# Attention: where the guard's checks of a blocked inverse stand, which engine copies a first column, and who writes two diagonal blocks

## The chip, the core and the metric

The program runs on one core of a Trainium2 chip. The metric is the device time of one execution in microseconds (us). The engines named below are TensorE (PE, with its weight loads PEld), VectorE (DVE), ScalarE (ACT), GpSimd (POOL) and SyncE (SP, which issues most of the DMAs). Each engine works through its own instructions in the order in which they stand.

## The reference

Three layers follow each other. The change lies in the first, a recurrence over 768 steps for 4 x 8 heads with a 40x40 state each; its outputs are routed, token by token, to one of 8 experts, and a dense layer with a leaky activation ends it.

```python
# _attn_ref: r, k, v, w, a, b are [4, 8, 768, 40]
for t in range(S):
    y[:, :, t] = np.einsum('bhd,bhde->bhe', rt, state)
    Sa = np.einsum('bhde,bhe->bhd', state, at)
    state_decay = state * wt[:, :, None, :] - np.einsum('bhd,bhe->bhde', Sa, bt)
    state = state_decay + np.einsum('bhd,bhe->bhde', vt, kt)
# _moe_ref: x is y as [3072, 320]
logits = x @ w_gate; expert_idx = np.argmax(logits, axis=1)   # gate = softmax at the argmax
out[mask] = gate_w[mask, None] * (np.maximum(x[mask] @ w1[e], 0.0) @ w2[e])   # for each expert e
# _moe2_ref
h = x @ w_in
return (np.maximum(h, 0.0) + alpha * np.minimum(h, 0.0)) @ w_out
```

## The kernel before

The recurrence is computed in chunks of 64 steps. Four chunks (256 steps) of two batches form a *group*; there are six groups, `os[0]` to `os[5]`. For a group, `prepare` loads w, k, b and a for a quarter of it at a time (four calls a group, 24 in all), takes products of the decays by two scans on DVE (lines 465 and 467, with a reciprocal at 466 between them), and scales k, b and a. The first column of the first scan's result, 104x8 numbers, is kept in `s0` for the step from one chunk to the next; a copy on ACT (line 471) does that. `products` multiplies the scaled tiles on PE (`lp`, line 494), and ACT copies the result into `l1` and `l2`. `inverse` then inverts the 64x64 triangular matrices of the group: their 32x32 diagonal blocks by 31 steps on DVE in the tile `ut` (lines 551 and 553), two transposes on DVE into `ttc` and `t11` (lines 573 and 576), and the blocks off the diagonal by two rounds of matmuls, `zp` (line 597) and `yp` (line 607). The result T is put together in the tile `tt`, a half of the group at a time. `diagonal` copies the diagonal blocks from `ttc` into `tt` (line 569, four instructions a half), on POOL, but on DVE for the first half of the first group. ACT copies `zp` into `z` (line 601) and `yp` into `tt` (line 610, "the copies of T"). The first group has eight small matmuls on a tile of ones ahead of each `zp` and each `yp` (`fill`).

A guard watches whether the numbers stay in a safe range. `check` squares a tile on ACT with an accumulator: one instruction and a short one that reads the accumulator. For each group `inverse` checks `ut` and then `l1`, ahead of the second half (lines 587 and 588); the first writes its squares over `ut`, the second into `ttc`. `ut` is also read by the transpose into `t11`, so its check waits for that.

The chunks themselves run in 48 *slots*, eight a group. In a slot, PE multiplies T into the sides (`pp`, line 649), ACT copies that (`pw`, line 651), PE makes `sa` (line 689), ACT and DVE copy it to `va` (lines 691 and 694), PE makes `yc` (line 705), DVE takes the next state `sm` from it (lines 709 and 710), PE transposes that (`tp`, line 716), and ACT copies it to `bds` (line 717). The next group's `prepare`, `products` and `inverse` are laid among the slots of the group before, by a table in `run`: a group's first half of T is needed in its first slot, its second half four slots on.

What stands where on each engine is decided by a scheduler that places instructions by modelled times, except in the first stretch, where DVE, POOL and ACT keep the order of the code (`manual_schedule`, closed by `self.region.close()`). `issue_after` tells the scheduler to place an instruction behind another.

Of the kernel before, what the change touches and what calls it, by code (L numbers as in the profile page):

```python
# [13 lines left out]
AF = mybir.ActivationFunctionType  # L14
ALU = mybir.AluOpType
# [273 lines left out]
class Attention:  # L289
# [148 lines left out]
    def prepare(self, o, pg):  # L438

        nc = self.nc  # L440
        nw = 2 * NCS * CW
        half, bb = divmod(pg, 2)
        p4 = slice(4 * bb, 4 * bb + 4)
        if pg == 0:
            o.s0 = self.p.tile([PP, 8, NCS], F32, name="s0", bufs=4)
            o.group, o.q, o.la, o.kbr = {}, {}, {}, {}
        if bb == 0:
            o.q[half] = self.p.tile([PP, 8, 2, CW], F32, name="q", bufs=5)
        kbs, abds = (self.kb_start, self.abd_start) if o.start else (self.kb, self.abd)
        wz, ra, kb, abd = (self.ringed(*n) for n in (("wz", self.wz), ("ra", self.ra), ("kb", kbs), ("abd", abds)))  # L450
        for q in range(2):
            r = slice(q * HQ, q * HQ + D)
            nc.sync.dma_start(wz[r], self.wP[o.bp, o.g, pg, q])
            nc.sync.dma_start(kb[r].rearrange("p a x t -> p (a x t)"), self.kbP[o.bp, o.g, pg, q])
            nc.sync.dma_start(ra[r].rearrange("p a t -> p (a t)"), self.aP[o.bp, o.g, pg, q])
        w3 = wz[:, :nw].rearrange("p (c t) -> p c t", t=CW)[:, :, 1:]
        s = self.pa.tile([PP, nw], F32, name="s", bufs=2)
        s3 = s.rearrange("p (c t) -> p c t", t=CW)
        qt = o.q[half][:, p4]
        qc = qt.rearrange("p a c t -> p (a c) t")  # L460
        if o.start:
            self.check(w3, self.pa.tile([P, 2 * NCS, C], F32, name="junk", tag="t4", bufs=3)[:PP], 1.24, self.mid)
        else:
            self.check(w3, qc[:, :, :C], 1.24, self.mid)
        nc.vector.tensor_tensor_scan(s[:, ::-1], wz[:, 1:][:, ::-1], self.d1s[:, ::-1], 0.0, ALU.mult, ALU.max)
        nc.vector.reciprocal(self.d1q.rearrange("p (c t) -> p c t", t=CW)[:, :, 0], s3[:, :, 0])
        nc.vector.tensor_tensor_scan(qt.rearrange("p a c t -> p (a c t)"), wz[:, :nw], self.d1q, 0.0, ALU.mult, ALU.max)  # L467
        for x in range(2):
            eng = nc.vector if o.start else nc.gpsimd
            eng.tensor_tensor(kb[:PP, :, x, :], kb[:PP, :, x, :], s3[:, :, 1:], op=ALU.mult)  # L470
        nc.scalar.copy(o.s0[:, p4, 2 * half:2 * half + 2], s3[:, :, 0].rearrange("p (a c) -> p a c", c=2))
        for q in range(2):
            r = slice(q * HQ, q * HQ + D)
            nc.gpsimd.tensor_tensor(abd[r, :, q * C:(q + 1) * C], ra[r], qc[r, :, :C], op=ALU.mult)  # L474
        o.group[pg] = abd.rearrange("p (a c) t -> p a c t", c=2), kb.rearrange("p (a c) x t -> p a c (x t)", c=2)
# [50 lines left out]
    def inverse(self, o):  # L526

        nc = self.nc
        l1, l2 = o.l1, o.l2
        o.tt = [self.ringed("tt", self.tt) for _ in range(2)]  # L530
        ut = self.ut0 if o.start else self.unit()
        ul = self.pa.tile([P, 32, 32], F32, name="ul", tag="t4", bufs=3)
        nc.vector.transpose(ul, l2.rearrange("p c u j -> p j (c u)"))
        yield
        for j in range(31):
            n, m = 31 - j, j + 1
            if o.start:
                if j == 0:
                    tmp = self.pa.tile([P, 1024], F32, name="tmp", tag="t4", bufs=3)
                col = ul[:, j, j + 1:]  # L540
            else:
                if j == 0:
                    bank = self.work("tmp", [P, 512], "mg")
                    tmp = bank[:, :256]
                if j in (0, 8, 16):
                    j0, j1 = j, (8, 16, 32)[j // 8]
                    part = bank[:, 256:256 + (j1 - j0) * (32 - j0)].rearrange("p (a b) -> p a b", b=32 - j0)
                    nc.scalar.copy(part, ul[:, j0:j1, j0:])
                col = part[:, j - j0, j + 1 - j0:]
            tv = tmp[:, :n * m].rearrange("p (a b) -> p a b", b=m)  # L550
            nc.vector.tensor_tensor(tv, col.unsqueeze(2).to_broadcast([P, n, m]),
                                    ut[:, j, :m].unsqueeze(1).to_broadcast([P, n, m]), op=ALU.mult)
            nc.vector.tensor_tensor(ut[:, j + 1:, :m], ut[:, j + 1:, :m], tv, op=ALU.subtract)  # L553
            if j % 2:
                yield

        lows = [slice(q * 64, q * 64 + 32) for q in range(2)]
        highs = [slice(q * 64 + 32, q * 64 + 64) for q in range(2)]

        def vacant(half):  # L560
            if not o.start:
                for lo, hi in zip(lows, highs):
                    nc.gpsimd.memset(o.tt[half][lo, :, :, hi], 0.0)

        def diagonal(half):
            for q in (1, 3, 0, 2):
                r = slice(32 * q, 32 * q + 32)
                eng = nc.vector if o.start and half == 0 else nc.gpsimd
                eng.tensor_scalar(o.tt[half][r, :, :, 32 * q:32 * q + 32], ttc[r, 2 * half:2 * half + 2], 1.0, 0.0, op0=ALU.mult, op1=ALU.add)

        vacant(0)
        ttc = self.t4("ttc")
        nc.vector.transpose(ttc.rearrange("p c u t -> p t (c u)"), ut)
        diagonal(0)
        t11 = self.t4("t11")
        nc.vector.transpose(t11.rearrange("p c u s -> p s (c u)"), ut.rearrange("p t s -> p s t"))
        yield

        pairs = [(c2, u) for u in range(8) for c2 in range(2)]
        out = lambda t, c2, q: t[c2 * 64:c2 * 64 + 32, :, q * 32:q * 32 + 32]  # L580
        heads = lambda t: t.rearrange("p (q s) -> p q s", q=2)
        wide = lambda t, c, u: t.rearrange("p c u j -> p (c u j)")[:, 32 * (8 * c + u):min(32 * (8 * c + u) + C, 1024)]
        for half in range(2):
            if half:
                vacant(1)
                diagonal(1)
                self.check(ut, ut, 0.01)
                self.check(l1.rearrange("p c u j -> p (c u) j"), ttc.rearrange("p c u t -> p (c u) t"), 0.01)
                yield
            tt = o.tt[half]  # L590
            zp = self.work("zp", [P, 8, C], "mg" if o.start or half == 0 else "w1")
            if o.start:
                self.fill(zp, 8)
            for c2, u in pairs:
                w = wide(l1, 2 * half + c2, u)
                high = heads(tt[:, c2, u])[:, :, 32:]
                nc.tensor.matmul(heads(zp[c2 * 64:c2 * 64 + w.shape[1], u]), lhsT=w, rhs=high, start=True, stop=True)
            z = self.z
            for c2 in range(2):
                for q, lo in enumerate(lows):  # L600
                    nc.scalar.copy(z[lo, c2, :, q * 32:q * 32 + 32], out(zp, c2, q))
            yp = self.work("yp", [P, 8, C], "mg" if o.start or half == 0 else "w1")
            if o.start:
                self.fill(yp, 8)
            for c2, u in pairs:
                w = wide(t11, 2 * half + c2, u)
                nc.tensor.matmul(yp[c2 * 64:c2 * 64 + w.shape[1], u], lhsT=w, rhs=z[:, c2, u, :], start=True, stop=True)
            for c2 in range(2):
                for q, (lo, hi) in enumerate(zip(lows, highs)):
                    nc.scalar.activation(tt[lo, c2, :, hi], out(yp, c2, q), AF.Copy, scale=-1.0)  # L610
            yield


# [767 lines left out]
```

## Time and profile before

| | |
|---|---|
| Device time, median of 3 runs | 1084.41 us (1084.05 to 1087.19) |
| The profiled execution | 1090.49 us, its span 1088.8 us |
| PE busy in the span | 980.7 us (90%) |
| DVE / ACT / POOL busy | 681.9 / 536.5 / 490.9 us |

The span is from the first to the last instruction of one execution. An engine is busy while an instruction of it runs, and idle while the next one waits; each wait is put down to the instruction that ended last before it, its releaser. The attention's inverse of the first group ends near 100 us, the 48 slots run to about 480 us, and the experts and the dense layer fill the rest.

### The profile page before, as it was taken

To read this page: it belongs to the slowest core of one execution; us is meant where nothing else is said; L and a number is where in the kernel's file an instruction comes from. 1 tells how busy PE (TensorE), PEld (TensorE's weight loads), DVE (VectorE), ACT (ScalarE), POOL (GpSimd) and SP (SyncE) were. 2 spreads that over 40 slices of the span, in tenths; PEclk is the share of its full clock that TensorE was granted. 3 is DMA by queue.
4 is the path that set the end of the run, shared out by engine and by line. 5 is a ranking of instruction groups with operands and counts; after the bars stand their busy time and mean duration, and the time that the engine had idled before them with its cause. 6 is when DMAs were issued, how large, how long until landed. Compare 5 with 4: busy or idle time off the path is not lost. (4 is left out here: it accounts for less than half of the span.)

```text
span 1088.8 us, 24353 instructions
## 1 busy us (share of the span) xinstructions
PE 980.7 (90%) x9213; PEld 871.9 (80%) x9213; DVE 681.9 (63%) x1493; ACT 536.5 (49%) x1303; POOL 490.9 (45%) x571
## 2 busy tenths in 40 slices
PE   2669987888879998887999999999999999999997
PEld 2557776777668777776899999899898988988986
DVE  9795968868978695556899753243444444344533
ACT  4657766686677777645677544421212222222211
POOL 7766677785867645320000003524435343534332
PEclk8669999999999999898999999999999999999999
DMA  4462323333323234427999643410000000000000
GB/s 121 103 204 72 93 73 81 90 77 83 89 77 84 55 68 105 111 55 262 324 332 321 212 149 106 124 46 7 19 25 25 25 25 25 26 25 25 25 1 28
DMA packets 128320, 103.33 MB, mean 95 GB/s; under 512 B 90564, under 2 KB 111044, under 8 KB 128196
## 3 DMA queue, kind: packets, MB, share of 16 engines
q1 hardware_dynamic: 125892, 93.83, 30.1%
q0 software_dynamic: 2304, 7.87, 2.3%
q8 instruction: 75, 1.23, 0.5%
q14 instruction: 49, 0.40, 0.1%
HBM read 79.39 MB, written 22.28 MB: 93 GB/s over the span
## 5 line engine op out<-in xcount | busy, mean ns | idle before, releaser
L234 POOL TENSOR_TENSOR gl<-g,gh 128x512 fp32r<-128x512 f32 x96 | 123.6, 1290 | 216.4 <-ACT gh L233 124.8
L233 ACT ACTIVATE gh<-g 128x512 fp32r<-128x512 f32 x96 | 60.8, 633 | 251.9 <-DVE g L1268 178.2
L1267 DVE TENSOR_SCALAR g<-ph,al 128x512 f32<-128x512 f32 x96 | 72.1, 751 | 160.1 <-POOL gl L234 77.6
L243 PE MATMUL ph<-x2thi,win 128*128 128x512 f32 x480 | 159.5, 397 | 0.0
L243 PE MATMUL po<-wout,gh 128*128 128x320 f32 x768 | 139.0, 310 | 0.0
L243 PEld LDWEIGHTS po<-wout,gh 128*128 128x128 f32 x768 | 122.0, 188 | 5.6
L243 PE MATMUL ph<-x2tlo,win 128*128 128x512 f32 x288 | 114.3, 397 | 0.0
L243 PEld LDWEIGHTS ph<-x2thi,win 128*128 128x128 f32 x480 | 88.6, 188 | 14.9
L243 PE MATMUL po<-we,hh 128*128 128x320 f32 (+1 forms) x480 | 92.5, 322 | 6.8 <-ACT hh L1137 6.1
L243 PE MATMUL ph<-xthi,we 128*128 128x448 f32 (+2 forms) x360 | 97.5, 342 | 0.1
L1076 POOL TENSOR_TENSOR win<-raw,win 128x1024 fp32r<-128x1024 f32 x4 | 9.6, 2406 | 185.3 <-ACT win L1074 185.2
L243 PEld LDWEIGHTS po<-we,hh 128*128 128x128 f32 (+1 forms) x480 | 75.9, 187 | 10.7 <-ACT hh L1137 6.7
L243 PE MATMUL po<-wout,gl 128*128 128x320 f32 x384 | 82.9, 312 | 0.0
L243 PE MATMUL ph<-xtlo,we 128*128 128x448 f32 (+2 forms) x216 | 73.7, 342 | 0.9 <-DVE xtlo L276 0.9
L494 PE MATMUL lp<-kb,abd 128*128 128x128 f32 x352 | 58.2, 309 | 17.2 <-POOL abd L474 10.3
L474 POOL TENSOR_TENSOR abd<-ra,q 40x512 f32<-40x512 f32 x44 | 61.4, 1396 | 22.4 <-DVE q L467 12.3
L243 PEld LDWEIGHTS ph<-xthi,we 128*128 128x128 f32 x360 | 66.5, 195 | 3.3 <-ACT xthi L273 0.2
L1268 DVE SCALAR_TENSOR_TENSOR g<-ph,g 128x512 f32<-128x512 f32 x96 | 66.3, 691 | 3.1
L243 PEld LDWEIGHTS po<-wout,gl 128*128 128x128 f32 x384 | 64.0, 188 | 3.0
L494 PEld LDWEIGHTS lp<-kb,abd 128*128 128x128 f32 x352 | 49.1, 212 | 21.6 <-POOL abd L474 10.8
L553 DVE TENSOR_TENSOR ut<-ut,tmp 128x31 f32<-128x31 f32 (+15 forms) x186 | 62.5, 336 | 3.6
L689 PE MATMUL sa<-vg,pw 128*64 128x104 f32 x768 | 57.2, 262 | 6.8 <-issue 4.6
(217 smaller groups left out, 2241.5 us busy)
## 6 DMA issues: line engine op xcount, KB each, us to landing
raw<-in_moe_w_dram SPq DMA_DIRECT2D x16, 512.0 KB
raw<-in_moe_w_dram SPq DMA_DIRECT2D x16, 480.0 KB
kb<-in_kbP_dram SPq DMA_DIRECT2D x44, 160.0 KB
r<-in_moe_w_in_dram SPq DMA_DIRECT2D x10, 512.0 KB
r<-in_moe_w_out_dram SPq DMA_DIRECT2D x10, 512.0 KB
xs_d<-tt SPq DMA_DIRECT2D x8, 560.0 KB
raw<-in_moe_w_dram SPq DMA_DIRECT2D x16, 256.0 KB
wz<-in_wP_dram SPq DMA_DIRECT2D x48, 81.4 KB
```

What stands on the lines that cost most here:

```text
L233: nc.scalar.activation(hi, src, AF.Copy)
L234: return lo_eng.tensor_tensor(lo, src, f32(hi), op=ALU.subtract)
L243: return nc.tensor.matmul(out, lhsT=lhsT, rhs=rhs, start=start, stop=stop)
L474: nc.gpsimd.tensor_tensor(abd[r, :, q * C:(q + 1) * C], ra[r], qc[r, :, :C], op=ALU.mult)
L494: nc.tensor.matmul(lp[:, i], lhsT=abd[:, i, c2, :], rhs=kb[:, i, c2, :], start=True, stop=True)
L553: nc.vector.tensor_tensor(ut[:, j + 1:, :m], ut[:, j + 1:, :m], tv, op=ALU.subtract)
L689: nc.tensor.matmul(sa[q * 64:q * 64 + 64, i], lhsT=x.pw[:, i, q * C:(q + 1) * C], rhs=x.vg[:, i, q, :], start=True, stop=True)
L1076: eng.tensor_tensor(wt[:, 3 + c, cs], raw, f32(wt[:, c, cs]), op=ALU.subtract)
L1267: nc.vector.tensor_scalar(g, ph, 0.0, al[:, f:f + 1], op0=ALU.min, op1=ALU.mult)
L1268: nc.vector.scalar_tensor_tensor(g, ph, 0.0, g, op0=ALU.max, op1=ALU.add)
```

## The change

The copy of the first column goes from ACT to DVE, between the reciprocal and the second scan. Of the four diagonal blocks of the first half of the first group, ACT writes two and DVE two. The two checks leave the start of the second half: the check of `ut` is placed behind the copies of T of the first half, that of `l1` behind those of the second, which now writes its squares over `l1`. The `fill` ahead of `yp` goes.

```diff
         nc.vector.reciprocal(self.d1q.rearrange("p (c t) -> p c t", t=CW)[:, :, 0], s3[:, :, 0])
+        nc.vector.tensor_copy(o.s0[:, p4, 2 * half:2 * half + 2], s3[:, :, 0].rearrange("p (a c) -> p a c", c=2))
         nc.vector.tensor_tensor_scan(qt.rearrange("p a c t -> p (a c t)"), wz[:, :nw], self.d1q, 0.0, ALU.mult, ALU.max)
...
-        nc.scalar.copy(o.s0[:, p4, 2 * half:2 * half + 2], s3[:, :, 0].rearrange("p (a c) -> p a c", c=2))
...
                 r = slice(32 * q, 32 * q + 32)
-                eng = nc.vector if o.start and half == 0 else nc.gpsimd
-                eng.tensor_scalar(o.tt[half][r, :, :, 32 * q:32 * q + 32], ttc[r, 2 * half:2 * half + 2], 1.0, 0.0, op0=ALU.mult, op1=ALU.add)
+                to, src = o.tt[half][r, :, :, 32 * q:32 * q + 32], ttc[r, 2 * half:2 * half + 2]
+                if o.start and half == 0 and q % 2:
+                    nc.scalar.copy(to, src)
+                else:
+                    eng = nc.vector if o.start and half == 0 else nc.gpsimd
+                    eng.tensor_scalar(to, src, 1.0, 0.0, op0=ALU.mult, op1=ALU.add)
...
-                self.check(ut, ut, 0.01)
-                self.check(l1.rearrange("p c u j -> p (c u) j"), ttc.rearrange("p c u t -> p (c u) t"), 0.01)
...
-            if o.start:
-                self.fill(yp, 8)
...
-                    nc.scalar.activation(tt[lo, c2, :, hi], out(yp, c2, q), AF.Copy, scale=-1.0)
+                    done = nc.scalar.activation(tt[lo, c2, :, hi], out(yp, c2, q), AF.Copy, scale=-1.0)
+            with self.tc.issue_after(done.ins):
+                src = l1.rearrange("p c u j -> p (c u) j") if half else ut
+                self.check(src, src, 0.01)
```

The scheduler lays all instructions anew, so the order moves beyond these lines. ACT in the first group, before, from the check of `ut` on (`s` is the first column, `tt_127` the first half of T):

```order
L434 ACTIVATE ut,checks_134<-ut 128x1024
L471 COPY s_1447<-s 104x4x2
L601 COPY z_120<-zp 32x8x32 x4
L434 ACTIVATE ttc,checks_134<-l_183 128x1024
L495 COPY l_617<-lp 128x128
L496 COPY l_618<-lp 128x128
L515 COPY kbr<-bp 128x320
L679 COPY vg_410<-rp 40x4x64 x2
L681 COPY rs<-rp 104x256
L471 COPY s_1447<-s 104x4x2
L610 ACTIVATE tt_127<-yp 32x8x32 x4
```

The same place now, from the two diagonal blocks on (line 609 holds the copies of T):

```order
L570 COPY tt_127<-ttc 32x16x32 x2
L603 COPY z_120<-zp 32x8x32 x4
L495 COPY l_608<-lp 128x128
L496 COPY l_609<-lp 128x128
L515 COPY kbr<-bp 128x320
L609 ACTIVATE tt_127<-yp 32x8x32 x4
L434 ACTIVATE ut,checks_134<-ut 128x1024
L521 ACTIVATE la<-ap 64x4x40 x2
```

Ahead of the copies to `z` two blocks of T stand instead of a check and a column; ahead of the copies of T a check, a column and the copies of `rp` are gone; behind them a check has come.

ACT at the end of a later group's inverse (the third), before:

```order
L434 ACTIVATE ut,checks_134<-ut 128x1024
L691 COPY va_409<-sa 64x4x40 x2
L515 COPY kbr<-bp 128x320
L601 COPY z_120<-zp 32x8x32 x4
L521 ACTIVATE la<-ap 64x4x40 x2
L717 COPY bds_417<-tp 104x208
L662 COPY vg_412<-rvp 64x4x64 x2
L434 ACTIVATE ttc,checks_134<-l_1482 128x1024
L495 COPY l_2583<-lp 128x128
L496 COPY l_2584<-lp 128x128
L610 ACTIVATE tt_128<-yp 32x8x32 x4
```

And now:

```order
L694 COPY va_409<-sa 64x4x40 x2
L515 COPY kbr<-bp 128x320
L603 COPY z_120<-zp 32x8x32 x4
L521 ACTIVATE la<-ap 64x4x40 x2
L720 COPY bds_417<-tp 104x208
L665 COPY vg_412<-rvp 64x4x64 x2
L609 ACTIVATE tt_128<-yp 32x8x32 x4
L434 ACTIVATE ut,checks_134<-ut 128x1024
L495 COPY l_2568<-lp 128x128
L496 COPY l_2569<-lp 128x128
L515 COPY kbr<-bp 128x320
L654 COPY pw_422<-pp 104x512
```

One check has gone from ahead of `va` and `z` to between the copies of T and the slot's `pw` (line 654); the check of `l1` has left this place. DVE at the end of the first group's inverse now:

```order
L577 STREAM_TRANSPOSE ttc<-ut 128x32x32
L580 STREAM_TRANSPOSE t_513<-ut 128x32x32
L573 TENSOR_SCALAR tt_127<-ttc 32x16x32 x2
L465 SCALAR_TENSOR_TENSOR s<-wz_106,d1s_117 104x520
L466 RECIPROCAL d1q_122<-s 104x8
L467 COPY s_1432<-s 104x4x2
L468 SCALAR_TENSOR_TENSOR q<-wz_106,d1q_122 104x520
```

Two blocks of the diagonal stand here where four stood, and the copy of the column has come ahead of the second scan, here and at each of the other calls of `prepare`.

## Rows read from the trace of the kernel before

**Rows 1.** Busy time by stretch: us, busy of each engine (instructions), PE clock, DMA share, GB/s.
```profile
0.00:77.25 77.25, 38.55 (x200) 32.92 (x201) 67.16 (x120) 40.76 (x101) 53.79 (x70) 0.71 0.51 151
77.25:102.80 25.55, 24.42 (x348) 21.19 (x349) 13.83 (x18) 17.09 (x53) 17.23 (x19) 0.89 0.21 58
102.80:475.00 372.20, 323.18 (x5222) 274.77 (x5220) 287.70 (x801) 263.07 (x762) 243.82 (x350) 0.98 0.34 83
```

**Rows 2.** Waits of PE from 102 to 475 us: us in total, times, longest.
```profile
PE tp L716 <- DVE sm L710: 15.9, 18, 1.9
...
PE yp L607 <- ACT z L601: 3.3, 3, 2.6
...
PE pp L649 <- ACT bds L717: 1.4, 1, 1.4
```

**Rows 3.** Timeline, end of the first inverse: start, us, instruction [idle before <-releaser].
```profile
71.20 1.95 DVE L573 STREAM_TRANSPOSE ttc<-ut 128x1024 f32<-128x1024 f32 x1
...
74.90 4.21 DVE L569 TENSOR_SCALAR tt<-ttc 32x512 f32<-32x512 f32 x4
...
77.25 1.97 PE L597 MATMUL zp<-tt,l 128*64 128x64 f32 x32 [7.29 <-DVE tt L569]
...
80.71 0.20 ACT L471 COPY s<-s 104x8 f32<-104x8 f32 x1 [4.69 <-DVE s L465]
80.82 1.51 ACT L601 COPY z<-zp 32x256 f32<-32x256 f32 x4
...
83.04 0.62 PE L243 MATMUL yp<-ones 128*128 128x128 bf16 x8
83.59 1.15 PE L607 MATMUL yp<-z,t 128*64 128x64 f32 x32
...
86.39 0.20 ACT L471 COPY s<-s 104x8 f32<-104x8 f32 x1 [0.61 <-DVE s L465]
86.50 1.54 ACT L610 ACTIVATE tt<-yp 32x256 f32<-32x256 f32 x4
```

**Rows 4.** Waits of ACT from 102 to 475 us.
```profile
ACT s L471 <- DVE s L465: 25.1, 13, 3.2
...
ACT ut L434 <- DVE t L576: 9.3, 4, 2.7
```

**Rows 5.** Timeline, ACT and PE at the end of the third group's inverse.
```profile
221.77 1.15 PE L597 MATMUL zp<-tt,l 128*64 128x64 f32 x32 [1.03 <-POOL tt L569]
...
222.10 1.06 ACT L434 ACTIVATE ut<-ut 128x1024 f32<-128x1024 f32 x1 [2.60 <-DVE t L576]
...
224.21 1.52 ACT L601 COPY z<-zp 32x256 f32<-32x256 f32 x4
...
226.21 1.11 PE L607 MATMUL yp<-z,t 128*64 128x64 f32 x32
...
227.26 1.06 ACT L434 ACTIVATE ttc<-l 128x1024 f32<-128x1024 f32 x1
...
228.74 1.54 ACT L610 ACTIVATE tt<-yp 32x256 f32<-32x256 f32 x4
...
231.46 0.58 ACT L651 COPY pw<-pp 104x512 f32<-104x512 f32 x1 [0.23 <-PE pp L649]
```

**Rows 6.** Durations by line: ns min/median/max, first and last start, forms.
```profile
L434 ACT ACTIVATE ut<-ut x6: 1008/1058/1059, 74.9 to 415.3; 128x1024 f32<-128x1024 f32 x6
L434 ACT ACTIVATION_READ_ACCUMULATOR ut<-ut x6: 185/186/194, 75.8 to 416.3; 128x1 f32 x6
L466 DVE RECIPROCAL d1q<-s x24: 153/196/207, 5.9 to 344.5; 104x8 f32<-104x8 f32 x24
L974 DVE TENSOR_SCALAR over<-sl x12: 151/222/457, 151.4 to 481.8; 128x2 f32<-128x2 f32 x12
L569 DVE TENSOR_SCALAR tt<-ttc x4: 739/1056/1305, 74.9 to 78.4; 32x512 f32<-32x512 f32 x4
L324 ACT COPY vv<-zero x2: 626/628/630, 34.4 to 35.8; 128x512 f32<-128x512 f32 x2
```

## The prediction

> **What bounds the kernel now.** I read the busy times by stretch first. Up to 77.25 us DVE is busy for 67.16 us of 77.25 and PE for only 38.55: the scans and the 31 steps of the first inverse on DVE set the pace. From there to 102.8 us PE is busy 24.42 of 25.55 us, so PE is nearly full. From 102.8 to 475 us no engine is: PE has 323.18 of 372.2 us, DVE 287.70, ACT 263.07 [rows 1]. In this stretch, the slots, each engine waits for another in turn. The waits of PE come second: the largest is for DVE's state `sm`, 15.9 us in 18 times; for ACT there are smaller ones, the copies to `z` 3.3 us and `bds` 1.4 us [rows 2]. So a stall on ACT costs something only where ACT stands between two matmuls that wait for it. The waits of ACT come third: 25.1 us in 13 times for the first scan, ahead of the copy of the column, and 9.3 us in 4 times for the transpose into `t11`, ahead of the check of `ut` [rows 4]. Both are instructions at the head of ACT's queue whose own result nobody needs soon; what stands behind them waits with them. Behind 480 us PE's matmuls are the chain, and the change does not touch them: what the attention gains or loses is carried to the end.
>
> **First group.** The transpose into `ttc` ends at 71.20 + 1.95 = 73.15 us, and `zp` starts at 77.25, behind DVE's first two blocks, which stand behind the second transpose [rows 3]. Now ACT writes these two, and it is idle then. The nearest row for such a copy is 0.63 us (128x512, half of whose lanes it needs) [rows 6], so two take 1.26 and `zp` may start near 74.5. But eight of the new DVE copies stand ahead of `ttc` (four calls of `prepare` for the first group, four for the second). The nearest row is the reciprocal on the same 104x8 numbers, 0.196 us [rows 6]: 8 x 0.2 = 1.6 us, all on the DVE path. `zp` comes 4.1 - 1.26 - 1.6, about 1.2 us, earlier. Then the copies to `z`: `zp` ends at 79.22, they start at 80.82, because a column copy waited 4.69 us for a scan: 1.6 us that go. `yp` ends at 84.74, the copies of T start at 86.50, again behind a column copy: 1.76 us that go [rows 3]. Together 4.5 us. PE can't give so much: in the stretch to 102.8 us it idles 25.55 - 24.42 = 1.1 us, and the two fills ahead of `yp` save 2 x 0.62 [rows 1, 3]. So the bound is 1.2 + 1.1 + 1.2 = 3.5 us. The check of `ut`, 1.06 + 0.19 = 1.25 us [rows 6], stands ahead of the first slot's `pw` now, and both halves of T ahead of the first `va`. I take -2.5 us, with 0 and -4.5 as ends. The fills had covered a wait of PE; `lp` and `bp`, which stand between `zp` and `yp` in the new order, are the cover that is left.
>
> **The ends of the five other inverses.** The one at 222 us shows the pattern. `zp` ends at 222.92; the check of `ut`, which had waited 2.60 us for the transpose, ends near 223.25, and `z` starts at 224.21, 1.29 us late. `yp` ends at 227.32; the check of `l1`, from 227.26, holds the copies of T until 228.74, 1.42 us late [rows 5]. With both checks gone T comes up to 2.7 us earlier. Then the check of `ut` stands between T and `pw`, which takes 1.25 us of it back: 1.45 us earlier at `pw`, and that only if PE, which is also full at these places, follows. At the other ends the lateness is smaller or PE's order sets `yp`. I take half, 0.7 us, five times: -3.5 us. The ends: -13.5 (2.7 each) and +6 (each check adds its 1.25 ahead of `pw` and what stood before it had been hidden).
>
> **The check of l1 behind the second half of T.** It does not vanish: 1.25 us now stand ahead of `va` or `bds` of the slot in which the second half is finished, five times, 6.3 us at most. Where a column copy waited at the same place, up to 3.2 us [rows 4], the room is there already. I take +1 us, from 0 to +6.3.
>
> **The column copies in the slots.** On ACT 13 waits of 25.1 us go [rows 4]. But what stands behind them (`bds`, `vg`, `pw`) mostly meets PE or DVE waiting for that same scan. Of PE's waits for ACT the row on `bds`, 1.4 us, is one that a column copy causes; the others are a few tenths. I take -1.5 us, from 0 to -6. On DVE 16 copies come, 16 x 0.2 = 3.2 us, between the reciprocal and the scan that `abd`, and so `lp`, wait for. DVE is busy for 287.70 of 372.2 us [rows 1]; I put half of it on the path: +1.6 us.
>
> The price of that copy is not shown. It is bounded by the reciprocal (0.196) below. Above, by rows in which a DVE instruction on SBUF data is stretched: the four blocks of 32x512 took 0.739 to 1.305 us, a 128x2 tensor_scalar 0.151 to 0.457 [rows 6]. I take 0.2, the row of the same shape; at 1.3 us the 16 copies would be 21 us and the eight ahead of `ttc` 10. The Trainium skill, in "SBUF — State Buffer", section "Who interferes with whom", says that a copy whose source and target lie in SBUF can take the second pair of ports, which VectorE shares with GpSimd, and that whichever of the two starts first blocks the other for its whole instruction. The spread of the four blocks agrees with it, and no run here shows a copy of 104x8. By it the sum would go the way of the fourth case below.
>
> **The sum.** -2.5 - 3.5 + 1 - 1.5 + 1.6 = -4.9 us. The profiled execution took 1090.49 us, 1.69 more than its span; that becomes 1085.6. The median of the runs shown is 6.08 us below the profiled execution, so the forecast for the median is 1079.5 us. The case's own range, with half to one and a half of the gain, is 1077 to 1082.
>
> **The rivals.**
> Second: more comes. If the slots are bound by the exchange between ACT and DVE, in which ACT waits for a scan and DVE for ACT's copies, then the ends of the inverses give their 1.45 us each in full (7.3), the first group its bound of 3.5, and the column copies 1.5 more: -12 us, 1072. For it: both rows of [rows 4] are larger than all of PE's waits for ACT. Against: PE's largest wait is for DVE's `sm` [rows 2], and DVE gets more work.
> Third: no change. The slots' chain goes through DVE's `sm` and through PE, which is busy for 87% of the stretch; what the ends of the inverses win is waited off at the next `sm`, and the check that now stands ahead of `pw` takes the rest. The first group's 2.5 us are met by the 3.2 us of DVE copies: 1084.4. Against: the first group's stretch is PE's, and the fills are simply gone.
> Fourth, slower: the new copy on DVE is held by POOL, which is busy for 243.82 of 372.2 us with instructions that read SBUF [rows 1]. At the median of the four blocks, 1.06 us [rows 6], each copy costs 0.86 us more than counted. In the 71 us ahead of `ttc` DVE is the path, so the eight give 6.9 us there; of the 16 others, 13.8 us, I put a quarter on the path, 3.4. With the -4.9 of the sum that is +5.4 us: 1089.8. It decides from a mean copy of about 0.6 us on. Against: the reciprocal just ahead of it on the same numbers is never above 0.207 us, and the scan behind it would meet POOL anyway, so that part of such a wait is only moved.
> That the change doesn't do what it says is ruled out for the order: both checks stand behind the copies of T, and no column copy is left on ACT.
>
> **How the numbers follow.** Forecast 0.45, second 0.13, third 0.22, fourth 0.20. What can be told from no change is about 0.3%, 3.3 us. The forecast lies at -4.9, so a part of it, 0.03, falls into "same": faster 0.55; same 0.23, with a little of the third case going either way; slower 0.22. The range takes in the second case and nearly all of the fourth: 1070 to 1090.
>
> **What would show it.** In the trace after: the two blocks on ACT near 0.6 us each and `zp` of the first group near 76 us; `z` straight behind `zp` and T straight behind `yp`, in all six groups; no wait of ACT ahead of a check; DVE copies near 0.2 us; the first `sm` 2 to 3 us earlier than now and the last near 5. The forecast is wrong if the DVE copies take 0.6 us or more, if `pw` behind the check comes later against T than it did, or if the first `sm` is earlier but the last is not.

## The result and the profile after

The changed kernel is slower. Six runs of it have a median of 1090.35 us (1087.92 to 1093.47), six of the kernel before 1085.70 us (1082.55 to 1089.43). The ratio is 1.0051, with a 95% interval of 1.003 to 1.0072. A second measurement, below, gives 1.0044. All ratios are taken over the fast runs of the two kernels and are not quotients of the medians, from which they differ by up to 0.17%. The forecast was 1079.5 us. The fourth case, the new DVE copy held by POOL, had 1089.8.

The two traces would tell the opposite: the profiled execution of before took 1090.49 us, more than any of its six timed runs, and that of after 1087.92 us, the least of its six. So what follows takes places and durations from the traces, and the price from the medians.

The busy times by stretch, of after, answer to [rows 1]; the columns are the same.

```profile
0.00:77.25 77.25, 38.30 (x200) 32.72 (x200) 67.89 (x125) 39.03 (x92) 49.20 (x67) 0.73 0.49 145
77.25:102.80 25.55, 23.34 (x325) 20.55 (x327) 14.10 (x21) 18.51 (x53) 20.07 (x20) 0.81 0.21 60
102.80:475.00 372.20, 325.58 (x5235) 277.87 (x5231) 291.58 (x816) 263.52 (x750) 248.52 (x352) 0.97 0.35 84
```

In the second stretch PE is busy for 1.08 us less than before, but that does not tell whether its work came earlier: the two fills that are gone had 0.62 us each, and a second trace of the kernel before (e8, below) has 23.42 us there. The timeline of after at the end of the first inverse, which answers to [rows 3], tells more.

```profile
73.89 1.91 DVE L577 STREAM_TRANSPOSE ttc<-ut 128x1024 f32<-128x1024 f32 x1
...
75.25 0.72 ACT L434 ACTIVATE q<-wz,mid 104x512 f32<-104x512 f32 x1 [1.94 <-DMA wz<-in_wP_dram]
...
76.90 1.24 ACT L570 COPY tt<-ttc 32x512 f32<-32x512 f32 x2
...
78.20 1.98 PE L599 MATMUL zp<-tt,l 128*64 128x64 f32 x32 [5.54 <-ACT tt L570]
...
80.22 1.52 ACT L603 COPY z<-zp 32x256 f32<-32x256 f32 x4 [2.08 <-PE zp L599]
...
82.30 0.85 DVE L467 COPY s<-s 104x8 f32<-104x8 f32 x1
...
83.62 1.98 PE L607 MATMUL yp<-z,t 128*64 128x64 f32 x32
...
85.64 1.53 ACT L610 ACTIVATE tt<-yp 32x256 f32<-32x256 f32 x4 [1.49 <-PE yp L607]
87.20 1.01 ACT L434 ACTIVATE ut<-ut 128x1024 f32<-128x1024 f32 x1
```

The handovers are as the edit meant them: `z` starts 0.04 us after `zp` ends (78.20 + 1.98), and T as closely behind `yp`. But `ttc` starts 2.69 us later than before. ACT's two blocks, 0.62 us each, wait another 1.1 us behind two checks of `q` that a DMA had held up. So `zp` starts 0.95 us later than before instead of 1.2 us earlier. In the second trace of the changed kernel (e1) the two blocks do not wait for a check, and `zp` starts at 76.95 us; but `ttc` is late there too, at 73.63.

The waits of ACT and of PE from 102 to 475 us, of after; they answer to [rows 4] and [rows 2].

```profile
ACT va L694 <- PE sa L692: 17.8, 32, 1.1
ACT l L495 <- PE lp L494: 13.3, 13, 1.4
ACT bds L720 <- PE tp L719: 11.5, 12, 2.4
```

```profile
PE tp L719 <- DVE sm L713: 18.7, 15, 3.3
...
PE yp L607 <- ACT z L603: 2.2, 4, 1.2
```

ACT's 25.1 us ahead of the column copy and 9.3 us ahead of the checks are gone. ACT now waits for PE instead. PE waits 18.7 us for DVE's `sm`, 2.8 us more than before; in the second traces it is 16.8 (e1) against 14.7 (e8). The durations, of after, which answer to [rows 6]:

```profile
L466 DVE RECIPROCAL d1q<-s x24: 152/198/207, 5.9 to 342.7; 104x8 f32<-104x8 f32 x24
...
L467 DVE COPY s<-s x24: 120/271/2449, 6.1 to 318.7; 104x8 f32<-104x8 f32 x24
...
L570 ACT COPY tt<-ttc x2: 614/616/618, 76.9 to 77.5; 32x512 f32<-32x512 f32 x2
```

The 24 DVE copies of 104x8 numbers take from 0.12 to 2.45 us, 10.59 us in all, a mean of 0.44. Eight of them, 4.95 us, lie ahead of `ttc`.

### The profile page after: what moved, and what is told of

It reads as the page before. It is cut to its first block, busy times and chain, and to the rows that moved or that the text cites. A ratio compares the mean times of both kernels' runs of the same rounds, so it can differ in the third digit from the quotient of the medians.

```text
span 1086.2 us, 24314 instructions
## 1 busy us (share of the span) xinstructions
PE 981.8 (90%) x9197; PEld 873.7 (80%) x9197; DVE 686.1 (63%) x1515; ACT 536.8 (49%) x1281; POOL 493.8 (45%) x571
## 3 DMA queue, kind: packets, MB, share of 16 engines
q8 instruction: 75, 1.23, 0.5%
## 4 chain that ended last, share of the span: by engine, by line
PE 50%; DMA 2%; DVE 1%; ACT 1%; SPq 0%; issue 0%; POOL 0%; DVEq 0%; ACTq 0%
PE ph L243 24%; PE po L243 24%; PE tr_ps L270 2%; DMA raw<-in_moe_w_dram 2%; DMA raw<-w_out 0%; ACT wout L1093 0%; DVE we L1094 0%; DMA xs_d<-xr,sli 0%; POOL wout L1094 0%; ACT we L1077 0%; SPq L1076 0%; DVE dec L216 0%; SPq L1055 0%; ACT hh L1140 0%; DVE xtlo L274 0%
## 5 line engine op out<-in xcount | busy, mean ns | idle before, releaser
L494 PE MATMUL lp<-kb,abd 128*128 128x128 f32 x352 | 60.7, 319 | 16.0 <-DVE s L467 9.5
L494 PEld LDWEIGHTS lp<-kb,abd 128*128 128x128 f32 x352 | 51.7, 222 | 20.1 <-POOL abd L474 10.7
L243 PEld LDWEIGHTS ph<-x2tlo,win 128*128 128x128 f32 x288 | 54.2, 188 | 9.5
```

The source lines that it names most:

```text
L243: return nc.tensor.matmul(out, lhsT=lhsT, rhs=rhs, start=start, stop=stop)
L494: nc.tensor.matmul(lp[:, i], lhsT=abd[:, i, c2, :], rhs=kb[:, i, c2, :], start=True, stop=True)
```

## Experiments

The theories were these. A: the column copy on DVE is the price, since it is held while POOL works. B: the checks cost it, since they now stand between T and `pw` or `va`. C: leaving out the filling products on `yp` costs PE's clock. D: it is scatter. Others (E to H) are named where they come in. Each run was timed in five rounds beside the kernel before, except e8, which ran once.

| run | what it is | median us | ratio to before | 95% interval |
|---|---|---|---|---|
| e1 | the changed kernel again | 1092.64 | 1.0044 | 1.0020 to 1.0067 |
| e2, e12 | before + column copy on DVE | 1096.98, 1098.59 | 1.0083, 1.0081 | 1.0053 to 1.0114, 1.0048 to 1.0113 |
| e3 | before + checks behind T | 1088.05 | 0.9997 | 0.9973 to 1.0022 |
| e4 | before + two blocks on ACT, no fill | 1092.75 | 1.0018 | 0.9991 to 1.0046 |
| e5, e13 | as e2, a reduction for the copy | 1087.97, 1091.02 | 1.0023, 1.0007 | 1.0001 to 1.0045, 0.9987 to 1.0026 |
| e6 | changed, a reduction for the copy | 1087.87 | 1.0014 | 0.9995 to 1.0033 |
| e7, e16 | changed, column copy on ACT | 1082.28, 1081.77 | 0.9976, 0.9975 | 0.9954 to 0.9997, 0.9953 to 0.9997 |
| e9 | as e2, copy in the first 8 only | 1094.10 | 1.0030 | 1.0008 to 1.0052 |
| e10 | as e2, copy in the last 16 only | 1093.81 | 1.0026 | 1.0003 to 1.0049 |
| e11, e17 | as e7, with the fill on `yp` | 1085.68, 1081.24 | 0.9950, 0.9977 | 0.9926 to 0.9975, 0.9958 to 0.9996 |
| e14 | changed, with the fill on `yp` | 1091.45 | 1.0000 | 0.9978 to 1.0023 |
| e15 | before without the fill on `yp` | 1082.63 | 0.9981 | 0.9959 to 1.0003 |

The medians of before lie between 1084.87 and 1090.93 us from one set of runs to the next, so only ratios are compared across sets.

### e1 to e4: again, and one edit at a time

e1, no edit:

> The changed kernel once more, unaltered, beside the kernel before on the same chip. Theory A (the cost is real and sits in the edits): again 3 to 7 us above the kernel before. Theory D (the ratio of the first six runs, 1.003 to 1.0072, is scatter from run to run): within 0.3%, that is within 3 us. A second trace also tells which stretches repeat: under A the first tt copy again starts about 73.9 us and the column copies on DVE again take a mean of about 0.4 us with one or more above 1 us.

e2, against before:

```diff
+        nc.vector.tensor_copy(o.s0[:, p4, ...], s3[:, :, 0]...)   # behind the reciprocal
-        nc.scalar.copy(o.s0[:, p4, ...], s3[:, :, 0]...)          # behind the kb products
```

> The kernel before with one edit only: the first column of s is copied on DVE between the reciprocal and the scan, not on ACT. Theory A (a DVE copy is held while POOL works, and it stands ahead of the scan): 3 to 6 us slower than the kernel before, mean copy above 0.35 us, the first tt copy 2 to 3 us later than 71.2 us. Theory B (the place of the checks costs it): no change, within 2 us. My prediction's own step: 1.5 us faster to 1.6 us slower, with copies of 0.2 us.

e3, against before:

```diff
-                self.check(ut, ut, 0.01)          # behind diagonal(1)
-                self.check(l1..., ttc..., 0.01)
+            with self.tc.issue_after(done.ins):   # behind the copies of T
+                self.check(src, src, 0.01)
```

> The kernel before with one edit only: the two checks stand behind the copies of T. Theory B (the check now lies between the copy of T and what ACT does next, pw and va): 2 to 5 us slower than the kernel before. Theory A: 1 to 4 us faster, since only the gain of the shorter end of the inverse is left (my prediction's step: 2.5 us faster), and the waits of the check for DVE's t (9.3 us before) are gone.

e4, against before:

```diff
+                if o.start and half == 0 and q % 2:
+                    nc.scalar.copy(to, src)
-            if o.start:
-                self.fill(yp, 8)
```

> The kernel before with one edit only: in the first group ACT writes two of the four diagonal blocks, and the filling products on yp are left out. Theory C (without the filling products PE's granted clock falls in 77 to 103 us, 0.81 against 0.89): 1 to 3 us slower, first sm later than 102.8 us. My prediction's step: 1 to 3 us faster, zp near 75 us. Theory A and theory B: within 2 us of the kernel before.

The slowdown repeats, so D falls. Of the single edits only the column copy is slower than before beyond its interval, by 9 us, which is more than the whole change and more than the 3 to 6 us of A. B falls but for its lowest edge: the checks alone give 0.9997, at most 1.0022, that is 2.4 us. In e3 the gain that A and the forecast expected is not seen; the forecast's 2.5 us lie just inside the interval. e4 does not tell.

### e5, e6, e12, e13: is it the copy's form, or its place in the order?

A reduction over an axis of one element writes the same column. The order of every engine's instructions stays that of the twin with the copy, row for row; only these 24 instructions differ. e5 and e13 are e2 with it, e6 is the changed kernel with it, e12 is e2 again.

```diff
-        nc.vector.tensor_copy(o.s0[:, p4, ...], s3[:, :, 0]...)
+        nc.vector.tensor_reduce(o.s0[:, p4, ...], s3[:, :, 0:1]..., axis=AX.X, op=ALU.max)
```

> As the run with the column copy alone on DVE, whose order on all five engines it keeps row for row, but the column is written by a reduction over an axis of one element instead of a copy. Theory A (the copy's own stalls beside POOL are the cost): the 24 instructions take 0.12 to 0.2 us each, worst below 0.4 us, the first tt copy starts 1.5 to 2 us earlier than the 73.15 us of the copy, and at least half of that run's 0.83% is gone: 1.000 to 1.004 of the kernel before. Theory E (the new order alone costs it, whatever the instruction takes): 1.006 to 1.010 again. Theory F (any instruction at that place is held, by what POOL does, not by the form of the copy): the reduction too has a mean above 0.35 us and one above 2 us.

> The changed kernel with the same exchange: a reduction writes the column, the order on all five engines is that of the changed kernel row for row. Theory A: the changed kernel's 1.0044 falls to 0.997 to 1.001 of the kernel before, since only the copy's stalls were dear. Theory E: 1.003 to 1.006 again.

> The column copy alone on DVE once more, now beside its reduction twin on the same chip, since the halves (1.003 and 1.0026, against 1.0023 with no copy) do not add up to the 1.0083 first measured. Theory A (the held copies are the price, some 0.6%): 1.006 to 1.009. Theory H (the first measurement was high, the copies cost about 0.1 to 0.3% and the new order the rest): 1.003 to 1.0055.

> Its twin with the reduction, same order on all engines. Theory A and theory H both: 1.000 to 1.0045 as before; what counts is the distance to the copy's run on the same chip: 0.4 to 0.7% by A, 0.1 to 0.3% by H.

The same stretch of the twins: first DVE and POOL of e12, with the copy.

```profile
35.52 2.28 POOL L376 MEMSET vg<- 128x832 f32 x3
36.48 0.17 DVE L466 RECIPROCAL d1q<-s 104x8 f32<-104x8 f32 x1
36.57 0.50 DVE L467 COPY s<-s 104x8 f32<-104x8 f32 x1
...
38.13 0.44 POOL L376 MEMSET sm<- 104x416 f32 x1
38.49 2.45 DVE L467 COPY s<-s 104x8 f32<-104x8 f32 x1
38.52 0.98 POOL L376 MEMSET pw<- 128x512 f32 x2
38.59 2.34 DVE L551 TENSOR_TENSOR tmp<-ul,ut 128x31 f32<-128x31 f32 x1
39.45 1.45 POOL L376 MEMSET yt<- 128x512 f32 x3
...
40.99 0.20 DVE L553 TENSOR_TENSOR ut<-ut,tmp 128x31 f32<-128x31 f32 x1
...
73.30 1.93 DVE L573 STREAM_TRANSPOSE ttc<-ut 128x1024 f32<-128x1024 f32 x1
```

Then the same of e13, with the reduction.

```profile
39.30 0.12 DVE L467 TENSOR_REDUCE s<-s 104x8 f32<-104x8 f32 x1
39.32 0.99 POOL L376 MEMSET pw<- 128x512 f32 x2
39.41 0.19 DVE L551 TENSOR_TENSOR tmp<-ul,ut 128x31 f32<-128x31 f32 x1
39.63 0.20 DVE L553 TENSOR_TENSOR ut<-ut,tmp 128x31 f32<-128x31 f32 x1
...
40.25 1.45 POOL L376 MEMSET yt<- 128x512 f32 x3
...
71.02 1.92 DVE L573 STREAM_TRANSPOSE ttc<-ut 128x1024 f32<-128x1024 f32 x1
```

The copy of 38.49 us starts beside a run of memsets on POOL and ends at 40.94 us, with the last of them (39.45 + 1.45 = 40.90). It holds up the step of the inverse behind it. Beside the same memsets the reduction takes 0.12 us and the step 0.19. Nor is this one place: of the 24 copies of e12, 14 take more than 0.2 us, and each of them ends 0.03 us after an instruction of POOL has ended; in after the same holds for 13. The copies up to 75 us and from there on, by the stretch view of line 467 on DVE (busy, count, PE clock, DMA share, GB/s), of e12 and then of e13:

```profile
0.00:75.00 75.00, 4.95 (x8) 0.79 0.50 151
75.00:475.00 400.00, 5.41 (x16) 0.95 0.33 80
```

```profile
0.00:75.00 75.00, 0.94 (x8) 0.72 0.52 154
75.00:475.00 400.00, 2.15 (x16) 0.95 0.33 79
```

The holds are 4.01 and 3.26 us, 7.27 us together. `ttc` starts at 73.30 us in e12 and at 71.02 in e13. On one chip, with one order, copy and reduction differ by 0.0081 - 0.0007 = 0.74% (with the root of the summed squares of both half-widths, 0.36 to 1.12%), that is 8 us of 1091. So E (the new order alone costs it), F (any instruction at that place is held) and H (the first measurement was high) fall as causes of that price, and A stands: the form of the instruction is dear, not its place. In the changed kernel the same exchange gives 0.0044 - 0.0014 = 0.30% (0.00 to 0.60%, across two sets), 3.3 us, a little less than A had said: e6 lies just above its 1.001. There the holds are 10.59 - 3.09 = 7.5 us; why only half of them shows in the time is not settled, but a part of them is only moved: both scans together, over all calls of `prepare`, take 71.08 us in after and 73.53 in e6.

The Trainium skill, in "SBUF — State Buffer", section "Who interferes with whom", says that a copy can take the port pair that VectorE shares with GpSimd and is then blocked while an instruction of GpSimd that started first has it, and that a reduction on trn2 never contends. The rows agree with both: 2.45 us against 0.12.

### e7, e8: the rest of the change

e7 is the changed kernel with the column copy back on ACT (e2's edit undone), e8 the kernel before, run once for a second trace.

> The changed kernel with the column copy back on ACT behind the kb products; the checks and the first group's edits stay. Theory A: 0.997 to 1.001 of the kernel before, because checks alone measured 0.9997 and the diagonal edit alone 1.0018. Theory G (the three edits hurt each other through the new order): above 1.003. My prediction's terms for these two edits, 5 us faster together: 0.995.

> The kernel before once more, for a second trace. If its stretches repeat, the first tt copy starts within 0.5 us of 71.2 us, the first sm within 1 us of 102.8 us and the last sm within 2 us of 466.1 us; what differs by more is no evidence between two kernels.

e7 beats both kernels, though by little the one before: its interval ends at 0.9997, and so does that of e16. G (the three edits hurt each other through the new order) falls. The end of the first inverse in e7, by its timeline:

```profile
72.83 1.24 ACT L570 COPY tt<-ttc 32x512 f32<-32x512 f32 x2 [0.83 <-DVE ttc L577]
...
74.13 1.97 PE L599 MATMUL zp<-tt,l 128*64 128x64 f32 x32 [4.55 <-ACT tt L570]
...
76.15 1.52 ACT L603 COPY z<-zp 32x256 f32<-32x256 f32 x4 [2.07 <-PE zp L599]
...
78.87 1.15 PE L607 MATMUL yp<-z,t 128*64 128x64 f32 x32
...
80.07 1.53 ACT L610 ACTIVATE tt<-yp 32x256 f32<-32x256 f32 x4 [0.16 <-PE yp L607]
...
99.33 0.32 DVE L713 TENSOR_TENSOR sm<-yc,s 104x160 f32<-104x160 f32 x1
```

Here the first group does what was forecast: T starts 6.4 us earlier than in [rows 3]. The first `sm` comes at 99.33 us (100.56 in e16), against 102.81 before and, in e8, 102.91. Yet ACT waits for the scan ahead of the column copy nearly as long as before [rows 4], by the waits of e7 from 102 to 475 us:

```profile
ACT s L471 <- DVE s L465: 20.3, 10, 2.6
```

e6, without these waits and without held copies, is 0.38% behind e7 (0.09 to 0.67%). So taking ACT's waits away gave nothing back. Whether the 0.38% is the price of the 24 reductions on DVE, 3.09 us in all, or of the order that the scheduler lays around them, no run tells. Of the marks of e8, the first `sm` repeats, `ttc` is at 70.17 us instead of 71.20, and the last `sm` at 460.63 instead of 466.12. So my 0.5 and 2 us were too narrow, and differences of some 5 us late in the slots are no evidence between two traces.

### e9, e10: which copies?

```diff
+        self.ncol = getattr(self, "ncol", 0) + 1; <copy> if self.ncol <= 8 else <reduction>   # e9; e10 the mirror
```

> Order as in the runs with the column alone on DVE, row for row on all engines. The first 8 of the 24 columns are written by the copy, the other 16 by the reduction, so the two runs of before bound it: 1.0023 with no copy, 1.0083 with 24. Theory A1 (the price lies ahead of the first ttc, where DVE has no gap and the copies stand 2.4, 0.8 and 0.7 us): first ttc near 73.1 us, first sm near 106 us, ratio 1.0045 to 1.007. Theory A2 (the price lies in the slots of the later inverses): first ttc still near 73.1 us, but the ratio at 1.002 to 1.004, since the delay is made up before the next inverse.

> The mirror of it: the first 8 columns by the reduction, the other 16 by the copy, same order. Theory A1: first ttc near 71.3 us, first sm near 103.6 us, ratio 1.002 to 1.0045. Theory A2: the same first ttc, ratio 1.005 to 1.008. If the two parts add up, this ratio and that of the first eight have 1.0106 as their sum less 1.

`ttc` starts at 73.34 us in e9 and at 70.72 in e10, as both theories said. The ratios, 1.003 and 1.0026, do not add up: less 1 they are 0.56% together, where the last expectation had 1.06%. Both are near the twin with the reduction (1.0023, 1.0007); their intervals end at 1.0052 and 1.0049, where those of the twin with all copies begin at 1.0053 (e2) and 1.0048 (e12). By its ratio e9 fits A2, and e10 fits A1, so each half seems to say that the price lies in the other. Where it arises stays open.

### e11, e14 to e17: the filling products

e11 and e17 are e7 with the fill put back, e14 is the changed kernel with it, e15 is before without it, e16 is e7 again.

```diff
+            if o.start:
+                self.fill(yp, 8)
```

> The changed kernel with the column copy on ACT (0.9976) and with the filling products on yp put back, so only the checks and ACT's two diagonal blocks are left of the change. Theory C (leaving the fill out costs PE's clock): 0.995 to 0.997. My prediction's step (the fill is worth nothing at that place): within 0.2% of 0.9976.

> The changed kernel with only the filling products on yp put back. Theory C (leaving them out costs PE's clock in the first group; with the column on ACT they were worth 0.9976 less 0.995): 1.001 to 1.003, that is 0.2% or more under the changed kernel's 1.0044. Without that price: 1.0035 to 1.0055.

> The kernel before with one edit only: the filling products on yp of the first group are left out. Theory C (they are worth 0.25 to 0.44%, as the pairs 0.9976 against 0.995 and 1.0044 against 1.000 say): 1.0015 to 1.005. My prediction's step (they are worth nothing there) : 0.9985 to 1.0015.

> The changed kernel with its column copy on ACT, without the fill, now on one chip with its twin that has the fill. Theory C: 0.2 to 0.45% above the twin. Without a price of the fill: within 0.15% of it.

> The twin with the fill, the fastest version so far (0.995): 0.993 to 0.997 of the kernel before, by theory C under its twin; if the fill has no price, both lie at 0.995 to 0.998.

In after's trace `yp` took 1.98 us at a granted clock of 0.66 (80 to 90 us), where before had 1.15 at 0.85. That did not repeat: in e1 `yp` took 1.38 us at 0.89. e11 and e14 then seemed to say that the fill is worth 0.26 and 0.44%. With the column on ACT, side by side on one chip, no worth of it is seen: 0.9975 without it and 0.9977 with it, each with some 0.2% either way; and left out alone from the kernel before it gives 0.9981. There C falls. `yp` without the fill took 1.15 us in e7 and 1.98 in e16, the same kernel. In the changed kernel itself C stays open: e14, with the fill, is 0.44% under e1 (0.11 to 0.77%, across two sets), no less than the 0.30% that the exchange of the copy gives there, and no run has the two side by side.

## Why the prediction was wrong, point by point

**The step that failed** is the price of the column copy on DVE: "I take 0.2, the row of the same shape". The reciprocal has that shape, and its place, but it is never held (0.152 to 0.207 us in after too), while the copy right behind it took up to 2.45, with a mean of 0.44. The shape was the wrong likeness: the form decides. The row that did show a hold, the four blocks of `tensor_scalar`, was in the text as the upper end, and the fourth case was built on it.

**The column copies on ACT**: I credited -1.5 us for the waits that go. e6 against e7 shows no gain, with 1 to 7 us the other way. The two column terms, +0.1 us in the sum with a further 1.6 us ahead of `ttc` inside the first group's term, are together +0.7% of the kernel: from 0.9976 (e7) to 1.0044 (e1), 7.4 us (0.36 to 1.00%, across two sets). With the fill in both, from e11 or e17 to e14, it is 0.50 or 0.23%, so the size in the changed kernel is not well known; alone, in e2 and e12, the copy cost 0.83 and 0.81%.

**The first group**, -2.5 us with a bound of 3.5: the stretch came out as forecast without the DVE copies (first `sm` 3.5 us earlier in e7, 2.3 in e16), but not with them: it is at 104.17 us in after, 1.4 us later than before, and at 102.56 in e1, 0.25 us earlier. Common to both is that `ttc` comes 2.4 to 2.7 us later; the eight copies ahead of it took 4.95 us in after and 4.25 in e1, not 1.6. ACT's blocks take 0.62 us as the row of 128x512 said. That they can come to wait for the checks of `q`, as in after, I had not seen; in e1 they do not. The 1.24 us credited to the two fills are not seen between e16 and e17.

**The ends of the other inverses**, -3.5 us, and the check of `l1`, +1: not found. The end of the third group's inverse in after, ACT and PE, answers to [rows 5]:

```profile
222.83 1.15 PE L599 MATMUL zp<-tt,l 128*64 128x64 f32 x32 [1.10 <-POOL tt L573]
...
224.03 1.52 ACT L603 COPY z<-zp 32x256 f32<-32x256 f32 x4 [1.49 <-PE zp L599]
...
226.81 1.15 PE L607 MATMUL yp<-z,t 128*64 128x64 f32 x32
...
228.01 1.54 ACT L610 ACTIVATE tt<-yp 32x256 f32<-32x256 f32 x4 [0.83 <-PE yp L607]
229.57 1.06 ACT L434 ACTIVATE ut<-ut 128x1024 f32<-128x1024 f32 x1
...
231.37 0.61 ACT L654 COPY pw<-pp 104x512 f32<-104x512 f32 x1
```

From the start of `zp` to `pw` it is 8.54 us, 1.15 less than before, near the 1.45 that I had worked out for this place. So the local gain is there. But the checks alone give 0.9997 (0.9973 to 1.0022): no gain is seen at the end of the program. The net -2.5 us of these two terms lies just inside that interval, so that it is ruled out is not shown either.

**The sum.** Checks, blocks and the fill left out are together 0.9976 and 0.9975 in e7 and e16, some -2.7 us (-0.3 to -5.0), where their terms gave -5.0. So the other edits were right in sign and about half as large, and the column copy's 7.4 us outweighs them.

**The fourth case** named the mechanism and nearly the time, 1089.8 us against 1090.35. Its point of decision was a mean copy of about 0.6 us. The measured mean is 0.44 (0.62 in the eight ahead of `ttc`). It decided all the same, because the gains it had to outweigh were smaller. That the time came out so near is in part luck: the case put the mean copy at 1.06 us and 10.3 us of the excess on the path, and set the -4.9 us of the sum against that; both were too large. It spoke of instructions of POOL that read SBUF, while the longest hold is beside memsets, which only write. Its counter-argument, that the scan behind would meet POOL anyway, holds at one place and fails at another. At 10.8 us the copy of e12 takes 0.84 us and the scan behind it 1.23; in e13 the reduction takes 0.12 and the scan 1.79, so there the wait is only moved. Beside the memsets of 39 us nothing else waits in e13.

## What to carry to other kernels

Price a new instruction by a row of its form beside the engine that may hold it, not by a row of its shape; when the trace has only one stretched neighbour, that row is the upper end, and the likely value lies between the two as soon as the path runs through the place (here 0.44 us, between 0.2 and 1.06). A long wait at the head of an engine's queue is worth only what its release gives the next engine, and moving the waiting instruction to a busier engine can cost more than the wait. Before trading work between engines for such a wait, look for a form on the new engine that its neighbour does not hold; here even that form stayed behind the copy left on ACT.

## What was not expected of the hardware

- A DVE copy of 104x8 numbers waited out a run of six memsets of POOL, 2.45 us in each of after, e1, e2 and e12 (2.43 to 2.45), though these only write. It does not always wait out a run: the copy of 36.57 us in e12 ended at 37.07, with the second of three memsets, though the third ran from 36.98 to 37.80.
- Every copy above 0.2 us in after, e1, e2 and e12 (54 of them) ended 0.026 to 0.032 us after the end of an instruction of POOL: memsets, `tensor_tensor` and forms of `tensor_scalar` all held it.
- A reduction over an axis of one element takes 0.110 to 0.168 us for the same numbers in all of e5, e6 and e13, less than ACT's copy (0.188 to 0.227 in e7).
- Two traces of one order (e5 and e13) have their last `sm` at 466.0 and 471.0 us: the spread from run to run is about as large as the whole effect.
